# Two transformer layers on one core: part of V and of the queries made inside attention, scores first, compact reciprocals

## The chip, the cores and the metric

The kernel runs on one core of a Trainium2 chip. The metric is the device time of one execution in microseconds; the median of several runs is compared.

## The reference

Four blocks follow each other on x of 2048 positions by 1024 features: linear attention (A), softmax attention (B), then A and B again with the same weights. Each block normalises x, projects it to Q, K and V for 32 heads of 32 features, attends, projects with `wo` and adds the result to x.

```python
x = x + _A_ref(_layernorm(x), A_wqkv, A_w_phi, A_wo)
x = x + _B_ref(_layernorm(x), B_wqkv, B_wo)
x = x + _A_ref(_layernorm(x), A_wqkv, A_w_phi, A_wo)
x = x + _B_ref(_layernorm(x), B_wqkv, B_wo)
# _B_ref, per head:
scores = jnp.einsum("bhqd,bhkd->bhqk", q, k) * (Dh ** -0.5)
p = _softmax(scores, axis=-1)
o = jnp.einsum("bhqk,bhkd->bhqd", p, v)
# _A_ref, per head, with phi = [softmax(x w_phi), softmax(-x w_phi)]:
kv = phi_k^T v;  o = (phi_q kv) / (phi_q sum(phi_k))
```

x and the weights are bf16.

## The kernel before

The kernel does not issue its instructions as it goes. Each step is recorded with `op(engine, cost, function, dependences, buffers, priority)`. A planner (`Sched.run`) then plays the steps through with a cost for each, and writes them out in the order in which it started them. On the chip every engine works through its own list in that order and waits at the head for what it needs. The planner gives an engine the ready step with the lowest priority number whose buffers can be allocated: SBUF buffers come from one arena (the tile `arena`), with a quota per class (`QUOTA`), PSUM banks from eight. It looks past at most 60 steps that can't be allocated, and at most 80 units of priority ahead (`WINDOW`). A turn of attention is 10 units. A DMA is planned with 0.55 us to issue and `2.0 + kb / 200` us to land. All but two DMAs are issued from SP.

x stays in SBUF, transposed (`xT`), as four chunks of 512 positions (`NC`). "Layer" in the code means an A block and the B block behind it; `last` is the second. There are eight head groups of four heads (`G`).

The stage ahead of each B attention does, chunk by chunk, the queries and output of A (`a_queries`, `a_out`), layernorm, K of head group 0 (`b_k`) and V of head groups 0 to 3 (`b_v`, column block `fc` 0, four tiles of 128 positions; ACT evicts them). These matmuls are plain ones, 128x128 by 512 columns (line 421).

Attention (`attention`) walks 32 turns, each a chunk of queries and a head group: first chunks 0 and 1 by group, then chunk 2, then chunk 3. A turn has 64 units of 128 keys by 512 queries. Three units make one step: three score matmuls on separate row groups of the array (line 1006) into one of two PSUM score areas (three banks each), then one exponential of 128x1536 on ACT into an `E` buffer (line 1012). Scores for step n+2 need the area that step n's exponential has read. Two units make one products step (line 1042): V and a column of ones against the exponentials, four column tiles at once, accumulated in bank 6. After each half turn DVE copies bank 6 to an SBUF tile `T` (line 1057).

Some pairs of units are taken off ACT and done as a polynomial on DVE (`exp_dve`, lines 944 to 966); `EXTRA` says in which turns, one or two pairs a turn.

The rest of B's projections are *fills*, matmuls in four column tiles on bank 7 alone (`FIL`; line 425), put between attention's steps, each evicted by DVE: K of groups 1 to 7 (`b_k`), V of groups 4 to 7 (`b_v`, lines 839 and 1186), queries (`b_q`, line 847), the output projection (`b_o`, and `b_last` in the second layer), and in the first layer the keys of the next A block (`a_keys`). The queries of chunks 2 and 3 are made early, during the turns of chunks 0 and 1, from the weights loaded for those; `q_away` writes them to memory (`qd`, line 865) and `q_back` reads them shortly before their turn (lines 871 to 873). Where PE would otherwise work less than 75% of a 3.4 us spell, the planner puts in filler matmuls with a zero weight (line 1253).

The denominators of a turn come out of the ones column, equal in 32 rows per head. Two DMAs of 64x512 bring them beside each other (lines 1083 and 1085), four reciprocals of 128x128 follow on DVE (line 1087), and two products of 64x512 write the normalised output (line 1091):

```python
rc = [op("DVE", 128 * 8 / 960 + 0.12, lambda b=b, d_v=d_v, r_v=r_v: nc.vector.reciprocal(
    out=r_v()[:, b * P:(b + 1) * P], in_=d_v()[:, b * P:(b + 1) * P]), [m1, m2], [d_b], prio)
    for b in range(4)]
```

The last turn of each attention has a way of its own (lines 1064 to 1082).

Of the kernel before, what the change touches and what calls it, by code (L numbers as in the profile page):

```python
# [10 lines left out]
ACT = mybir.ActivationFunctionType  # L11
ALU = mybir.AluOpType
# [8 lines left out]
C512 = 512  # L21
# [11 lines left out]


class Op:
    __slots__ = ("eng", "dur", "lat", "fn", "bufs", "prio", "mode", "ndep", "out", "t", "start", "seq", "accum")

    def __init__(self, eng, dur, lat, fn, bufs, prio, mode, seq):
        self.eng, self.dur, self.lat, self.fn, self.bufs = eng, dur, lat, fn, bufs
        self.prio, self.mode, self.seq = prio, mode, seq  # L40
        self.ndep, self.out, self.t, self.start, self.accum = 0, [], 0.0, None, None


LAT = {"PE": 0.25, "ACT": 0.2, "DVE": 0.1, "POOL": 0.2, "SP": 2.0, "AQ": 2.0}
# [3 lines left out]
class Sched:  # L48
# [96 lines left out]
    def run(self):  # L145
# [20 lines left out]
        started = {}  # L166
        for o in self.ops:
            if o.ndep == 0:
                heapq.heappush(ready[o.eng], (o.prio, o.seq, o))
        t, left, order = 0.0, len(self.ops), []  # L170
        while left:
            moved = False
            for e in engines:
# [1 line left out]
                    continue  # L175
                skipped = []
                pick = None
                while ready[e] and len(skipped) < 60:
                    item = heapq.heappop(ready[e])
                    if item[0] <= todo[front] + WINDOW and self._alloc(item[2].bufs):  # L180
                        pick = item[2]
                        break
                    skipped.append(item)
                for s in skipped:
# [43 lines left out]
            if moved:  # L228
                continue
            if not events:  # L230
                stuck = [(o.prio, o.eng, [(b.cls, b.at) for b in o.bufs]) for e in engines for _, _, o in ready[e]][:8]
                raise AssertionError(f"nothing can start at {t:.1f}: {left} left, {stuck}, live {self.live}")
            t = events[0][0]
            while events and events[0][0] <= t + 1e-9:
                _, _, o, own = heapq.heappop(events)
                if not own:
                    for b in o.bufs:
                        b.left -= 1
                        if b.left == 0:
                            self._release(b)  # L240
                for x in o.out:

                    if own != (x.eng == o.eng and x.eng not in ("SP", "AQ")):
                        continue
                    x.ndep -= 1
                    if x.ndep == 0:
                        heapq.heappush(ready[x.eng], (x.prio, x.seq, x))
        self.end = t
        return order

# [4 lines left out]
LONG = {"kT", "v", "slab", "slabk", "xn", "xn1", "kvacc", "kvm", "zm", "wnat"}  # L255
MODEST = {"slabk", "xn1", "e1", "vp1", "pkf", "lnw1", "w2o"}
QUOTA = {"pk": 3, "pv": 2, "kv": 1, "ln": 2, "mm": 2, "cmp": 2, "bc": 4, "num": 1, "wt": 4, "fil": 2,
         "e": 6, "vp": 6, "e1": 4, "vp1": 4, "E": 5, "q2": 3, "kt": 3, "w2": 8, "w2o": 3, "oT": 26, "T": 4, "den": 2,
         "lnt": 6, "lnw": 2, "lnw1": 1, "eq": 8, "ns": 4, "cw": 6, "hl": 6, "oc": 2, "slab": 7, "slabk": 3, "fin": 4,
         "rs": 8, "pkf": 1, "part": 8, "w2r": 1,  # L260
         "xs": 1, "xu": 2, "xg": 2, "xx": 2, "E1": 3}
SPELL = 3.4
KEEP = 0.75
# [3 lines left out]
POW2_0 = 0.998010015430466  # L267
POW2_C = (-2.753493604392706, 3.611980637904819, -2.738565741928622)
LEAD = 5.0
EXTRA = (lambda i: [(i % 2, 2)] if 12 <= i < 17 else [],  # L270
         lambda i: [(0, 2), (1, 2)] if 16 < i < 30 and i % 4 else [(i % 2, 2)] if 8 <= i < 30 else [])


def act_us(n):
    return n / 1200 + 0.064


def dve_us(n):
    return n / 960 + 0.15
# [6 lines left out]
def kernel(  # L286
# [83 lines left out]
    wdq_v = wd_q[:].rearrange("(po pi) f -> pi po f", pi=P)  # L370
    wdk_v = wd_k[:].rearrange("(po pi) f -> pi po f", pi=P)

    qd = dram_p.tile([P, 2 * G * C512], BF16, tag="qd")
    qd_v = qd[:].rearrange("p (c g n) -> p c g n", c=2, g=G)
    xd = dram_p.tile([P, 3 * PO * C512], BF16, tag="xd")
# [206 lines left out]
    def flat(deps):  # L582
        r = []
        for d in deps:
            if isinstance(d, (list, tuple)):
                r.extend(flat(d))
            elif d is not None:
                r.append(d)
        return r
# [74 lines left out]
                            flat([last, kv_last.get((fc, lo))]), [pb, kv_b], pr))  # L664
                kv_last[(fc, lo)] = adds

    def mmg2(pb, pv, lhs, rhs, d1, d2, bufs, prio, lo=0, hi=4, more=False):

        last = None
        cols, us, mode = kind(pb)  # L670
        for i in range(lo, hi):
            def fn(i=i):
                for po in (2 * i, 2 * i + 1):
                    mm(pv(), lhs(po), rhs(po), po == 2 * lo, po == 2 * hi - 1 and not more, cols)
            last = op("PE", 2 * us, fn, [last] + flat([d1[i] if d1 else None, d2[i] if d2 else None]),
                      [pb, *bufs], prio, mode=mode)
        return last

# [154 lines left out]
                        in_=kv()[64 * pp:64 * pp + 64, 256 * hf:256 * hf + 256]),  # L833
                    [cp], [kb, k_b], kb=32))

    def evac(eng, dst, src, dep, bufs, prio):
        if eng == "ACT":
            return op("ACT", act_us(512), lambda: nc.scalar.copy(out=dst(), in_=src()), [dep], bufs, prio)
        return op("DVE", dve_us(512), lambda: nc.vector.tensor_copy(out=dst(), in_=src()), [dep], bufs, prio)  # L839

    def b_q(g, c, prio, w, banks):
        wb, ww, wd = w
# [29 lines left out]
            dma(prio, lambda: nc.sync.dma_start(out=q_v()[64:128, 1, :], in_=src[0:64]), [away], [q_b], kb=64),  # L872
            dma(prio, lambda: nc.sync.dma_start(out=q_v()[0:64, 1, :], in_=src[64:128]), [away], [q_b], kb=64)]

    def b_v(fc, c, t, prio, w, vT, banks, eng):
        wb, ww, wd = w
        xb, xv, fin = xnB[c]
        ts = slice(t * P, (t + 1) * P)
        pb, pv = ps("fil", banks)
        m = mmg2(pb, pv, lambda po: xv()[:, po, ts], lambda po: ww()[:, po, :], fin, wd, [xb, wb], prio)  # L880
        v_b, v_v, done = vT[(fc, c)]
        done[t] = evac(eng, lambda: v_v()[:, t, :], pv, m, [pb, v_b], prio)

    def b_o(ft, c, prio, w, oT, banks, part=None, lo=0, hi=4):

# [85 lines left out]
    def attention(base, kT, vT, q_of, gate, extra):  # L971
# [16 lines left out]
        while i < len(units):  # L988
# [14 lines left out]
            def sfn(grp=grp, s_v=s_v):  # L1003
                for x, (qc, g, pp, d, j) in enumerate(grp):
# [4 lines left out]
                        rhs=q_of[(qc, g)][1]()[r, (pp + j // 2) % 2, :],  # L1009
                        start=True, stop=True, tile_position=(32 * j, 0))  # L1010
            so = op("PE", 0.24, sfn, deps + (gate if n == 0 else []), [s_b, *bufs], prio - 2, mode="r")
            ex = op("ACT", act_us(w * C512), lambda s_v=s_v, e_v=e_v, w=w: nc.scalar.activation(  # L1012
                out=e_v()[:, 0:w * C512], in_=s_v(), func=ACT.Exp, scale=4 * math.log(2)),
                [so], [s_b, e_b], prio - 3)
# [6 lines left out]
        if True:  # L1021
            for qc, g in turns:
                T = []
                end = (qc, g) == turns[-1]
                for pp in range(2):
                    a_b, a_v = ps("acc", [(6,)])
                    last = None
                    for d in range(8):
                        prio = base + 10 * pos[(qc, g)] + 5 * pp + 0.5 * d
                        for u in range(2):  # L1030
# [17 lines left out]
                            ebs = [e_of[us[0]][0]]  # L1048
                            if e_of[us[1]][0] is not ebs[0]:
                                ebs.append(e_of[us[1]][0])  # L1050
                            last = op("PE", 0.225, fn, flat([last, ex_of[us[0]], ex_of[us[1]], v_done[kc % 4]]),
                                      [a_b, v_b, *ebs], prio - 1, mode="c")
                            last.accum = (d, u) != (7, 1)
                    if end and pp:
# [9 lines left out]
                if end:  # L1064
# [15 lines left out]
                        [ln], [o_b, l_b, a_b], prio))  # L1080
                    oTs[qc][g] = (o_b, o_v, s)
                    continue
                m1 = dma(prio, lambda d_v=d_v, T=T: nc.sync.dma_start(out=d_v()[hi_, :], in_=T[0][1]()[hi_, :]),
                         [T[0][2]], [d_b, T[0][0]], kb=128)
                m2 = dma(prio, lambda d_v=d_v, T=T: nc.sync.dma_start(out=d_v()[lo_, :], in_=T[1][1]()[lo_, :]),
                         [T[1][2]], [d_b, T[1][0]], kb=128)
                rc = [op("DVE", 128 * 8 / 960 + 0.12, lambda b=b, d_v=d_v, r_v=r_v: nc.vector.reciprocal(  # L1087
                    out=r_v()[:, b * P:(b + 1) * P], in_=d_v()[:, b * P:(b + 1) * P]), [m1, m2], [d_b], prio)
                    for b in range(4)]
                o_b, o_v = sb("oT", C512)  # L1090
                s = [op("DVE", dve_us(512), lambda a=a, b=b, k=k, o_v=o_v, r_v=r_v, T=T: nc.vector.tensor_tensor(
                    out=o_v()[a, :], in0=T[k][1]()[a, :], in1=r_v()[b, :], op=ALU.mult),
                    rc, [o_b, r_b, T[k][0]], prio)
                    for k, (a, b) in enumerate(((lo_, hi_), (hi_, lo_)))]
                oTs[qc][g] = (o_b, o_v, s)
        return oTs, so

# [25 lines left out]
    for layer in range(2):  # L1123
# [39 lines left out]
        for c in range(NC):  # L1163
            pr = second + 20 * c
            o_b, o_v = sb("oc", G, C512)
            oc = (o_b, o_v, {})
            for hf in range(2):
                a_queries(c, hf, pr + 5 * hf, wq_s, state, oc)
            a_out(c, pr + 22, wo_s, oc)
            xnB[c] = layernorm(c, pr + 23, ANY)  # L1170
            b_k(0, c, pr + 42, wk0, kT, ANY, "ACT")
            if c == 0:
                q_of[(0, 0)] = b_q(0, 0, pr + 42.5, wq0, ANY)
            for t in range(TB):
                b_v(0, c, t, pr + 43 + 0.1 * t, bv_s[0], vT, ANY, "ACT")
        gate = []
        at = second + 130

# [5 lines left out]
        for c in range(NC):  # L1184
            for t in range(TB):
                b_v(1, c, t, at + 4.5 * (4 * c + t) + 2, bv_s[1], vT, FIL, "DVE")
        for g in range(G):
            pr = at + 10 * pos[(0, g)]
            w = slab("w2", pr - 11, B_w[:, :, g * P:(g + 1) * P], P) if g else wq0
            for qc in range(NC):  # L1190
                if qc < 2:
                    if qc or g:
                        q_of[(qc, g)] = b_q(g, qc, pr + 10 * qc - 8, w, FIL)
                else:
                    away = q_away(g, qc, pr + 2 + 6 * (qc - 2), w, FIL)
                    q_of[(qc, g)] = q_back(g, qc, at + 10 * pos[(qc, g)] - 12, away)
# [92 lines left out]
```

## Time and profile before

| | us |
|---|---|
| median of 3 runs (2509.66 to 2510.57) | 2510.38 |
| the profiled execution's own time | 2511.27 |
| its span, first to last instruction | 2509.5 |
| PE, ACT, DVE busy | 2368.6, 2145.4, 1468.5 |
| exponentials of the first attention, first start and last end | 357.6 to 1343.8 |
| exponentials of the second attention | 1566.4 to 2497.5 |

In the profile, PE is TensorE's matmuls, PEld its weight loads, DVE VectorE, ACT ScalarE, SP the engine that issues the DMAs. L1012 is line 1012 of the kernel before. Matmuls are pipelined, so a busy PE is not PE at its peak; a matmul of 512 columns shows some 0.38 us, but the next one starts 0.22 us after it. Rows of waits give who waited, for whom, the total us, the number of times and the longest.

### The profile page before, as it was taken

Reading aid. Unit: us, or ns where it says so; the run is one execution under the profiler, and the core shown is the slowest. Engines: PE = TensorE matmul, PEld = TensorE weight load, DVE = VectorE, ACT = ScalarE, POOL = GpSimd, SP = SyncE. Lnnn points to the kernel's source line nnn. Section 1 sums busy time; section 2 is a strip of 40 time slices with the busy share of each in tenths; the row PEclk is TensorE's granted clock in tenths of the full one; section 3 lists DMA queues with packets and bytes.
Section 4 is the critical chain, followed back from the end, with each engine's and each line's share of the span. In section 5 each row is a group of like instructions: output and inputs, shape, how many; then the busy total and the mean of one; then the engine's idle time right before and its main releaser. Section 6 shows DMA issues by size and latency. Waiting matters only on the chain.

```text
span 2509.5 us, 62924 instructions
## 1 busy us (share of the span) xinstructions
PE 2368.6 (94%) x27872; PEld 893.4 (36%) x27872; DVE 1468.5 (59%) x2003; ACT 2145.4 (85%) x1897; POOL 26.1 (1%) x72
## 2 busy tenths in 40 slices
PE   7999999999999999999999999999999999999998
PEld 4443433333333333333333444333333333333333
DVE  6997653333356345654646766333356578687854
ACT  6335558999999999999996465699999999999998
POOL 0000000000000000000000000000000000000000
PEclk9999999999999999999999999999999999999999
DMA  9110012111121222222323001111121100110000
GB/s 219 33 44 1 22 21 48 35 36 44 41 62 42 56 54 69 77 66 69 114 65 116 1 5 38 36 36 35 40 62 27 35 27 27 29 33 27 25 25 27
DMA packets 185282, 117.39 MB, mean 47 GB/s; under 512 B 103344, under 2 KB 175024, under 8 KB 184240
## 3 DMA queue, kind: packets, MB, share of 16 engines
q1 hardware_dynamic: 183952, 111.26, 16.7%
q8 instruction: 218, 3.57, 0.6%
q10 hardware_dynamic: 1056, 2.10, 0.3%
q14 instruction: 56, 0.46, 0.1%
HBM read 62.46 MB, written 15.73 MB: 31 GB/s over the span
## 4 chain that ended last, share of the span: by engine, by line
ACT 46%; PE 31%; issue 12%; DVE 8%; SPq 1%; DMA 1%; ACTq 0%; DVEq 0%
ACT arena L1012 43%; PE psum L421 14%; PE psum L425 5%; PE psum L1042 5%; PE psum L1006 4%; DVE arena L616 1%; SPq L456 1%; PE psum L1253 1%; PE psum L780 1%; ACT arena L612 1%; DVE arena L625 1%; DVE arena L963 1%; DVE arena L662 1%; DVE arena L510 1%; DVE arena L514 1%
## 5 line engine op out<-in xcount | busy, mean ns | idle before, releaser
L1012 ACT ACTIVATE arena<-psum 128x1536 bf16<-128x1536 f32 x1342 | 1812.4, 1566 | 50.5 <-PE psum L1006 43.7
L1042 PE MATMUL psum<-arena 128*32 128x512 bf16 x4096 | 699.0, 385 | 11.6 <-ACT arena L1012 8.4
L1042 PE MATMUL psum<-arena,ones_bf 128*32 128x512 bf16 x4096 | 700.3, 386 | 0.0
L1006 PE MATMUL psum<-arena 32*128 32x512 bf16 x4022 | 522.8, 383 | 74.6 <-ACT arena L1012 68.3
L425 PE MATMUL psum<-arena 128*32 128x512 bf16 x8256 | 576.3, 380 | 4.9 <-DVE arena L625 1.3
L421 PE MATMUL psum<-arena 128*128 128x512 bf16 x2032 | 474.2, 383 | 18.1 <-DVE arena L514 5.4
L1006 PEld LDWEIGHTS <-arena 32*128 32x128 bf16 x4022 | 163.4, 91 | 574.8 <-issue 564.9
L421 PEld LDWEIGHTS <-arena 128*128 128x128 bf16 x2032 | 193.6, 98 | 265.8 <-issue 47.6
L425 PEld LDWEIGHTS <-arena 128*32 128x32 bf16 x8256 | 212.3, 96 | 209.8 <-issue 53.9
L1042 PEld LDWEIGHTS <-arena 128*32 128x32 bf16 x4096 | 165.8, 94 | 271.6 <-issue 246.5
L1087 DVE RECIPROCAL arena<-arena 128x128 f32<-128x128 f32 x248 | 212.9, 913 | 44.7 <-DMA arena<-arena 44.4
L1253 PE MATMUL psum<-xT,zero 128*32 128x512 bf16 x2712 | 218.5, 382 | 0.0
L839 DVE CAST arena<-psum 128x512 bf16<-128x512 f32 x112 | 77.3, 690 | 238.5 <-PE psum L425 238.1
L1042 PEld LDWEIGHTS <-ones_bf 128*32 128x32 bf16 x4096 | 158.4, 94 | 62.7 <-issue 50.8
L1057 DVE COPY arena<-psum 128x512 f32<-128x512 f32 x126 | 86.8, 689 | 157.3 <-PE psum L1042 155.6
L963 DVE SCALAR_TENSOR_TENSOR arena<-arena 128x1024 f32<-128x1024 f32 x111 | 135.6, 1222 | 2.3
L612 ACT ACTIVATE arena<-psum 128x512 bf16<-128x512 f32 x80 | 42.8, 600 | 86.1 <-PE psum L421 57.8
L742 ACT ACTIVATE arena<-psum 128x512 bf16<-128x512 f32 x128 | 69.8, 597 | 41.5 <-PE psum L421 32.0
L625 DVE TENSOR_TENSOR arena<-psum,arena 128x1024 bf16<-128x1024 f32 x64 | 78.3, 1224 | 39.6 <-PE psum L425 35.5
L510 DVE TENSOR_TENSOR arena<-xT,arena 128x1024 f32<-128x1024 bf16 x64 | 77.9, 1219 | 35.2 <-ACT arena L499 34.8
L1253 PEld LDWEIGHTS <-zero 128*32 128x32 bf16 x2712 | 70.3, 97 | 64.5 <-issue 16.8
L514 DVE TENSOR_TENSOR arena<-arena 128x1024 bf16<-128x1024 f32 x64 | 77.4, 1223 | 23.9 <-ACT arena L504 22.6
(100 smaller groups left out, 1428.3 us busy)
## 6 DMA issues: line engine op xcount, KB each, us to landing
arena<-arena SPq DMA_DIRECT2D x124, 128.0 KB, 2.2
arena<-in_A_wqkv_dram SPq DMA_DIRECT2D x10, 1024.0 KB, 5.5
arena<-in_B_wqkv_dram SPq DMA_DIRECT2D x32, 256.0 KB, 3.1
arena<-arena SPq DMA_DIRECT2D x256, 32.0 KB, 1.9
arena<-in_B_wo_dram SPq DMA_DIRECT2D x32, 256.0 KB, 3.0
arena<-wd_k SPq DMA_DIRECT2D x8, 1024.0 KB, 5.7
arena<-in_A_wo_dram SPq DMA_DIRECT2D x4, 1024.0 KB, 7.1
arena<-in_B_wqkv_dram SPq DMA_DIRECT2D x4, 1024.0 KB, 5.4
```

Source lines behind the costliest of these rows:

```text
L421: nc.tensor.matmul(out_, lhsT=lhsT, rhs=rhs, start=start, stop=stop, skip_group_check=True)
L425: nc.tensor.matmul(out_[ks, :], lhsT=lhsT[:, ks], rhs=rhs, start=start, stop=stop, tile_position=(0, 32 * k), skip_group_check=True)
L510: s1 = op("DVE", dve_us(1024), lambda pr=pr, w_v=w_v: nc.vector.tensor_tensor(out=w_v(), in0=xT[:, pr, csl(c)], in1=m_v().unsqueeze(1).to_ ...
L514: fin.append(op("DVE", dve_us(1024), lambda pr=pr, w_v=w_v: nc.vector.tensor_tensor(out=xv()[:, pr, :], in0=w_v(), in1=r_v().unsqueeze(1). ...
L625: ml = op("DVE", dve_us(1024), lambda vpv=vpv, wv_=wv_, sv=sv: nc.vector.tensor_tensor(out=wv_()[:, :, :, 0:DH], in0=vpv().rearrange("p (h ...
L963: last = [op("DVE", dve_us(1024), lambda i=i, c=c: nc.vector.scalar_tensor_tensor(out=x_v(), in0=(x_v() if i else g_v()), scalar=c, in1=g_ ...
L1006: nc.tensor.matmul(out=s_v()[:, x * C512:(x + 1) * C512], lhsT=kT[g][1]()[r, pp, d * P:(d + 1) * P], rhs=q_of[(qc, g)][1]()[r, (pp + j // ...
L1012: ex = op("ACT", act_us(w * C512), lambda s_v=s_v, e_v=e_v, w=w: nc.scalar.activation(out=e_v()[:, 0:w * C512], in_=s_v(), func=ACT.Exp, s ...
L1042: nc.tensor.matmul(out=a_v()[col:col + 32, :], lhsT=v_v()[:, kc % 4, o:o + DH] if what == 0 else ones_bf[:], rhs=ev()[:, x * C512:(x + 1) ...
L1057: cp = op("DVE", dve_us(512), lambda t_v=t_v, a_v=a_v: nc.vector.tensor_copy(out=t_v(), in_=a_v()), [last], [a_b, t_b], prio - 4)
L1087: rc = [op("DVE", 128 * 8 / 960 + 0.12, lambda b=b, d_v=d_v, r_v=r_v: nc.vector.reciprocal(out=r_v()[:, b * P:(b + 1) * P], in_=d_v()[:, b ...
L1253: nc.tensor.matmul(psum[32 * k:32 * k + 32, 6 * C512:7 * C512], lhsT=zero[:], rhs=xT[:, 0, 0:C512], start=False, stop=False, tile_position ...
```

## The change

In the planner, a step can be marked `first`; such steps go ahead of all others on their engine, whatever their priority. All score steps but the first two of each attention are marked. The planner now looks past 400 steps instead of 60. `E` gets six buffers instead of five.

In the second layer, V of head groups 2 and 3 (the upper 256 columns of column block 0) is no longer made in the stage ahead of attention but as fills of 256 columns, evicted by DVE; head groups 0 and 1 stay. Queries of chunks 2 and 3 are made by `b_q` shortly before their turn, with a weight load of their own, and don't go through memory. The first layer keeps both as they were.

In both layers the denominators are compacted: two DMAs pick one row of 512 per head into a 128x16 tile, one reciprocal is taken, the result goes to a memory scratch `rd`, and one DMA reads it back with each of the four rows repeated over 32 partitions. `EXTRA` is changed: pairs on DVE go from 5 to 10 in the first layer and from 32 to 34 in the second.

```diff
@@ Sched.run
-                heapq.heappush(ready[o.eng], (o.prio, o.seq, o))
+                heapq.heappush(ready[o.eng], (not o.first, o.prio, o.seq, o))
...
-                while ready[e] and len(skipped) < 60:
+                while ready[e] and len(skipped) < 400:
...
-         "e": 6, "vp": 6, "e1": 4, "vp1": 4, "E": 5, "q2": 3, ...
+         "e": 6, "vp": 6, "e1": 4, "vp1": 4, "E": 6, "q2": 3, ...
...
-EXTRA = (lambda i: [(i % 2, 2)] if 12 <= i < 17 else [],
-         lambda i: [(0, 2), (1, 2)] if 16 < i < 30 and i % 4 else [(i % 2, 2)] if 8 <= i < 30 else [])
+EXTRA = (lambda i: [(0, 2), (1, 2)] if 12 <= i < 17 else [],
+         lambda i: [(0, 2), (1, 2)] if 16 <= i < 30 else [(i % 2, 2)] if 10 <= i < 16 else [])
@@ attention
             so = op("PE", 0.24, sfn, deps + (gate if n == 0 else []), [s_b, *bufs], prio - 2, mode="r")
+            so.first = n >= 2
...
-                m1 = dma(prio, lambda d_v=d_v, T=T: nc.sync.dma_start(out=d_v()[hi_, :], in_=T[0][1]()[hi_, :]),
-                         [T[0][2]], [d_b, T[0][0]], kb=128)
-                m2 = dma(prio, lambda d_v=d_v, T=T: nc.sync.dma_start(out=d_v()[lo_, :], in_=T[1][1]()[lo_, :]),
-                         [T[1][2]], [d_b, T[1][0]], kb=128)
-                rc = [op("DVE", 128 * 8 / 960 + 0.12, ... for b in range(4)]
+                c_b, c_v = sb("cden", 16, dt=F32)
+                at_d = rd_v[len(gone)]
+                gone.append((qc, g))
+                m = [dma(prio, lambda k=k, c_v=c_v, T=T: nc.sync.dma_start(
+                    out=c_v()[64 * k:64 * k + 64, :],
+                    in_=T[k][1]()[64 * (1 - k):64 * (1 - k) + 64:32, :].rearrange("r (s c) -> r s c", c=16)),
+                    [T[k][2]], [c_b, T[k][0]], kb=4) for k in range(2)]
+                rc = op("DVE", 0.27, lambda c_v=c_v: nc.vector.reciprocal(out=c_v(), in_=c_v()), m, [c_b], prio)
+                aw = dma(prio, lambda c_v=c_v, at_d=at_d: nc.sync.dma_start(
+                    out=at_d.rearrange("h (s c) -> (h s) c", c=16), in_=c_v()), [rc], [c_b], kb=8)
+                bk = dma(prio, lambda r_v=r_v, at_d=at_d: nc.sync.dma_start(
+                    out=r_v(), in_=at_d.unsqueeze(1).to_broadcast([4, 32, C512])), [aw], [d_b], kb=256)
...
-                    rc, [o_b, r_b, T[k][0]], prio)
+                    [bk], [o_b, r_b, T[k][0]], prio)
@@ stage ahead of attention, and fills
-                b_v(0, c, t, pr + 43 + 0.1 * t, bv_s[0], vT, ANY, "ACT")
+                b_v(0, c, t, pr + 43 + 0.1 * t, bv_s[0], vT, ANY, "ACT", (0,) if last else (0, 1))
...
                 b_v(1, c, t, at + 4.5 * (4 * c + t) + 2, bv_s[1], vT, FIL, "DVE")
+                if last:
+                    b_v(0, c, t, at + 1.5 * (4 * c + t) + 3, bv_s[0], vT, FIL, "DVE", (1,))
...
+                elif last:
+                    pq = at + 10 * pos[(qc, g)]
+                    q_of[(qc, g)] = b_q(g, qc, pq - 14, slab("w2", pq - 20, B_w[:, :, g * P:(g + 1) * P], P), FIL)
                 else:
                     away = q_away(g, qc, pr + 2 + 6 * (qc - 2), w, FIL)
                     q_of[(qc, g)] = q_back(g, qc, at + 10 * pos[(qc, g)] - 12, away)
```

`b_v` and `mmg2` take the half of the columns and its share of the planned cost; the products wait for the half that holds their head group.

## The prediction

> **What bounds the kernel now.** I read the busy time by stage first, split at the edges of the two attentions (357 to 1346 us and 1566 to 2497 us). Columns: stretch, length, then busy time of PE, PEld, DVE, ACT, POOL, the granted clock, DMA.
>
> ```profile
> 392.00:617.00 225.00, 219.73 (x3122) 77.45 (x3125) 78.25 (x107) 218.50 (x163) 0.00 (x0) 1.00 0.16 39
> ...
> 1346.00:1566.00 220.00, 213.99 (x1122) 90.95 (x1121) 155.76 (x233) 115.09 (x193) 2.59 (x8) 0.98 0.07 21
> ...
> 1601.00:1769.00 168.00, 164.72 (x2356) 58.41 (x2360) 57.52 (x79) 161.92 (x121) 0.00 (x0) 1.00 0.17 40
> ...
> 2030.00:2497.00 467.00, 435.34 (x6122) 152.39 (x6122) 335.05 (x408) 465.47 (x347) 0.00 (x0) 1.00 0.10 26
> ```
>
> Late in attention ACT is busy 465.5 of 467 us; between the attentions it is busy for half the time and PE for 214 of 220. So two engines take turns as the bound: PE in the projections, ACT in attention. DVE bounds neither. The same stretches for line 1012, the exponential, alone (ACT busy, count):
>
> ```profile
> 392.00:617.00 225.00, 218.01 (x162) 1.00 0.16 39
> 617.00:900.00 283.00, 282.81 (x211) 1.00 0.20 52
> 900.00:1305.00 405.00, 372.82 (x274) 1.00 0.25 74
> ...
> 1601.00:1769.00 168.00, 161.73 (x120) 1.00 0.17 40
> 1769.00:2030.00 261.00, 255.23 (x191) 0.99 0.15 39
> 2030.00:2497.00 467.00, 465.47 (x347) 1.00 0.10 26
> ```
>
> Undisturbed, 211 exponentials take 283 us: 1.34 us each. At that pace the six rows need 217, 283, 367, 161, 256 and 465 us. Row three also holds 24 us of other ACT work (its ACT busy time over all lines is 396.56). What is left is ACT's lost time: 8, 0, 14, 7, 5 and 2 us. That is all that a better order inside attention can win. The view of waits after 1601 us names the late side:
>
> ```profile
> ACT arena L1012 <- PE psum L1006: 7.0, 11, 1.3
> ACT arena L1012 <- DMA qd<-arena: 3.6, 1, 3.6
> ```
>
> Scores are late, and once the write of a far query is. The timeline gives PE's rates (start, length, line, count; the last matmul's own 0.38 or 0.22 us is taken off):
>
> ```profile
> 131.56 0.85 PE L644 MATMUL psum<-arena 128*128 128x132 bf16 x12
> ...
> 1448.05 5.90 PE L421 MATMUL psum<-arena 128*128 128x512 bf16 x26
> ```
>
> 5.52/25 = 0.22 us (0.216 in longer rows) per 512 columns, 0.63/11 = 0.057 per 132. A straight line between them gives 0.109 for the new 256 columns (bounds 0.057 and 0.216). A step of attention's four column tiles costs the same 0.216, and going from scores to those and back about 0.1 each way.
>
> **Part by part.** The sum is made against this execution: span 2509.5, its time 2511.27, so 1.8 outside; the median of the runs is 2510.38, 0.9 below it.
>
> *Exponentials.* Pairs done on DVE rise from 37 to 44; each takes two of three units off ACT. The programs hold 1340 full and 2 one-unit exponentials before, 1336 and none after. ACT saves 4 x 1.34 + 2 x 0.75 (mean of the short form) = 6.9, less what a short one hides under its neighbour: **-6.5** (-6.9 to -6.3). Four go from the first attention.
>
> *V and its stage.* 128 matmuls of V (16 tiles x 8) halve: 128 x (0.216 - 0.109) = 13.7 us less PE work between 1346 and about 1600, and 16 ACT evictions go from 587 ns to something between 250 and 587. The other half returns as 128 four-tile steps inside attention: 128 x 0.109 = 14.0 us, its 16 evictions on DVE (0.25 to 0.69 each). PE has no slack early there: filler matmuls (line 1253), put in where PE lacks work, take only 5.3 of the 168 us after 1601. So I did not take the 13.7 whole, but summed PE's work in the order of both programs, from the last score group of the first attention to the 126th of the second: 398.6 us before, 386.4 after (plain matmuls 195.6 to 182.0, fills 69.6 to 75.2, attention's products 51.4 to 48.8, fillers 3.3 to 1.5, the rest unchanged). That is **-12**; the first three blocks of 21 groups come to 58, 30 and 30 us of PE for 28 of ACT, so the second attention begins slower than now. Bounds -4 (V was covering the chain of layernorm) and -16 (waits inside shrink too).
>
> *Queries of chunks 2 and 3.* 16 x 8 x 0.216 = 27.6 us of fills move from the first to the second half of the second attention, where fillers take 99 of 467 us: hidden; without that cover it would cost up to 27.6. Sixteen writes and 48 reads through memory go, 16 slab loads of 256 KB and 32 swaps come. The 3.6 us wait for such a write goes, and with it a stretch at half clock (1856 to 1867 us had 0.69 granted): **-4** of the 5 us lost in 1769 to 2030 (0 to -5).
>
> *Scores first, deeper search, sixth E buffer.* They can only win the lost time above. PE already waits for ACT before scores:
>
> ```profile
> L1006 PE MATMUL psum<-arena 32*128 32x512 bf16 x4022 | 522.8, 383 | 74.6 <-ACT arena L1012 68.3
> ```
>
> so where ACT is full this changes nothing. Early in the first attention PE's order sums to 3.5 us less over the first 168 groups (238.7 to 235.2): **-4** of 8 (0 to -8). In 900 to 1305, 8.2 of the 14 us are waits for scores; half of that, **-4** (+3, if products and keys come late instead, to -10). Late in the second: **-1** (0 to -2).
>
> *Compact reciprocals.* Per turn, 62 times, four reciprocals (3.65 us) become one of 128x16 (between 0.15, the smallest DVE rows, and 0.353, its 128x32 form: 0.25). DVE loses 62 x 3.4 = 211 us and gets 7 x 9.0 = 63 from the new pairs (lines 949 to 966). DVE is not the bound, so this wins nothing itself. But two copies become a chain of two small copies, the reciprocal, a write and a broadcast read back, 108 more issues on SP in all (739 to 847), and the two products then wait at DVE's head. The near rows:
>
> ```profile
> arena<-arena SPq DMA_DIRECT2D x124, 128.0 KB, 2.2
> ...
> arena<-in_B_wqkv_dram SPq DMA_DIRECT2D x32, 256.0 KB, 3.1
> ...
> arena<-in_B_wqkv_dram SPq DMA_DIRECT2D x4, 1024.0 KB, 5.4
> ...
> qd<-arena SPq DMA_DIRECT2D x32, 128.0 KB, 1.8
> ```
>
> Write and read take 0.35 + 1.8 + 0.48 + 3.1 = 5.7 us by the like rows (issue times from the same lines). The planner orders DVE for 0.55 + 2.04 + 0.55 + 3.28 = 6.4, so DVE should seldom stand; behind the products in its queue wait the fill bank's eviction and the T copy, then PE's next fill, then scores, and ACT has up to two scored groups (2.7 us) in hand. Now DVE stands 44.4 us for such copies, unnoticed. **+3** for one or two reads that meet the 1 MB weight loads and land 5 us late, less the cover (0 to +12, five of them).
>
> The Trainium skill ("DMA: Bandwidth & Descriptors", How many engines (k), under the section on the semaphore's 16) speaks against this read: the slowest dimension of either side sets how many of the 16 queues work, and the source has 4 rows there. That would put 64 KB on each of 4 queues, as the 1 MB load does on 16, so an estimate by it is 5.4 us in place of 3.1 and 8.0 for the trip: 1.6 us later than ordered, still inside the cover, and the sum would stay. No run shown has a read of this shape.
>
> **Sum.** -6.5 - 12 - 4 - 4 - 4 - 1 + 3 = -28.5: span 2481.0, with 1.8 outside 2482.8, and 0.9 less for the median: **2482**.
>
> **Rivals.**
> *The reciprocal's trip holds DVE (slower).* It decides once write and read pass 6.4 + 2.7 = 9.1 us, that is a read over about 6.5. For: 1 MB loads reach 7.2, one 128 KB write took 7.9, and with few fills one eviction stands right behind the products. Against: like sizes land in 3.1. If the read took 8 us throughout, each of 62 turns would be 1.5 us beyond the cover, 93 us, and PE's waits would bring half clock: 2482 + 90 = 2572 (2530 if half the turns pay). The Trainium skill's rule of 4 queues, above, gives 5.4 by itself, short of that point. Chance 0.11.
> *The projection stage is a chain.* If layernorm's ACT and DVE steps, not PE, end last, V's half buys 2 us instead of 12: 2492. Against: PE is busy 136.88 of 137 us between 1428 and 1565. 0.12.
> *Scores first does not do what it says*, since in-order PE and two score banks already set the pace: the 4 + 4 + 1 fall away: 2491. For: 68.3 us of score waits for ACT. 0.13.
> *All lost time goes*, at the far bounds: about 2466. For: the rows of waits that must vanish come to 8.2 + 7.0 + 3.6 us. 0.08.
> *Gains and new waits cancel*, 2507 to 2513: 0.03.
> The forecast itself, 2472 to 2490: 0.53.
>
> **Numbers.** Bounds added up: best -6.9 - 16 - 5 - 8 - 10 - 2 = -48, 2462; worst -6.3 - 4 + 0 + 0 + 3 + 0 + 12 = +5, 2514. That leaves out the first rival and little else. No change means within 0.2%, 5 us, about what a measurement of this kernel can tell. Below 2505: 0.53 + 0.12 + 0.13 + 0.08, less 0.03 for their upper ends = 0.83; within 0.03; above 0.14.
>
> **What would show it.** Right: the stage between the attentions some 20 us shorter, the second attention's first 126 exponentials no faster, exponentials 1336 at 1.34 us, the wait on qd gone, ACT's waits for scores below 15 us in all. Wrong: DVE's products waiting long for the read with PE waiting for DVE; a read landing over 6 us; gaps of PE in the projections.

## The result, and the profile after

The changed kernel takes **2857.66 us** (median of 4 runs, 2850.91 to 2860.57) against 2510.02 of the kernel before in the same session (2509.13 to 2510.57). The ratio is 1.1382 [1.1361, 1.1402]: 348 us slower, where 28 us faster was forecast. Its profiled execution has a span of 2854.8 us.

The busy time by stage of the changed kernel, in the columns of the prediction (length, PE, PEld, DVE, ACT, POOL, granted clock, DMA):

```profile
392.00:617.00 225.00, 195.83 (x2681) 67.08 (x2680) 48.07 (x74) 192.71 (x142) 0.00 (x0) 0.96 0.13 34
617.00:900.00 283.00, 235.51 (x2903) 74.28 (x2897) 113.90 (x152) 231.96 (x171) 0.00 (x0) 0.90 0.15 40
...
1520.00:1722.00 202.00, 191.15 (x1029) 84.90 (x1046) 141.76 (x215) 107.44 (x182) 2.58 (x8) 0.98 0.09 26
...
2030.00:2497.00 467.00, 383.56 (x4732) 122.09 (x4731) 213.44 (x274) 381.55 (x279) 0.00 (x0) 0.90 0.12 32
```

No engine is full any more inside attention. In the last row ACT is busy 381.6 of 467 us, where it was 465.5, with PE at 383.6. The stage between the attentions (third row) is the part that came out as forecast: 202 us, from the start of the last exponential to that of the next, for 223 before. The exponentials themselves are not slower (a mean of 1473 ns, 1566 before). The page's groups show where the time lies (busy us and mean ns, then idle time before them and what ended it). First the exponentials of the kernel before, then exponentials and score matmuls of the changed one:

```profile
L1012 ACT ACTIVATE arena<-psum 128x1536 bf16<-128x1536 f32 x1342 | 1812.4, 1566 | 50.5 <-PE psum L1006 43.7
```

```profile
L1023 ACT ACTIVATE arena<-psum 128x1536 bf16<-128x1536 f32 x1336 | 1829.9, 1473 | 389.6 <-DMA arena<-arena 267.5
L1015 PE MATMUL psum<-arena 32*128 32x512 bf16 x4008 | 555.3, 405 | 313.1 <-ACT arena L1023 307.2
```

ACT stands idle 389.6 us before its exponentials (50.5 in the kernel before), and 267.5 of that ends with a DMA from the arena to the arena. An exponential reads PSUM and writes an `E` buffer; none of its data passes through such a DMA. The line whose DMA it is, asked for by itself, names the culprit. Line 1098 is the pair of compact copies, and these are the instructions that waited for it (us, times):

```profile
L1098 SPq DMA_DIRECT2D arena<-arena x124: 507/549/624, 401.4 to 2815.6; - x124
...
  ACT arena L1023: 267.5, 118
  DVE arena L1102: 68.1, 29
  DVE arena L842: 63.1, 20
```

Only line 1102, the reciprocal, has business with that copy. The exponentials and line 842, DVE's eviction of K and V, write other buffers of the arena. The views of waits, of the engines and of the DMA queue, show both halves:

```profile
ACT arena L1023 <- DMA arena<-arena: 267.5, 118, 7.8
```

```profile
SPq L1098 <- ACT arena L1023: 80.1, 89, 3.9
```

In 89 cases the copy is issued only when the exponential ahead of it has ended, and in 118 the next exponential starts only when the copy has landed. The timeline shows one such stop, SP first, then ACT:

```profile
704.58 0.56 SPq L1098 DMA_DIRECT2D arena<-arena  x1
```

```profile
699.08 5.48 ACT L1023 ACTIVATE arena<-psum 128x1536 bf16<-128x1536 f32 x4
706.51 5.48 ACT L1023 ACTIVATE arena<-psum 128x1536 bf16<-128x1536 f32 x4 [1.96 <-DMA arena<-arena]
```

ACT ends at 704.56, the copy is issued at 704.58, and ACT starts again 1.96 us later. The compact copies are barriers for other buffers of the arena. In the instruction lists of the two programs the same can be counted without a run: 118 exponentials of the changed kernel wait for the copy issued directly ahead of them, with no other exponential between. In the kernel before, the exponentials that wait for line 1083 or 1085 have at least five others between, as buffers that are used again must have.

### The profile page after: what moved, and what is told of

Same layout as the page of the kernel before. It is cut to its first block, busy times and chain, and to the rows that moved or that the text cites. A ratio compares the mean times of both kernels' runs of the same rounds, so it can differ in the third digit from the quotient of the medians.

```text
span 2854.8 us, 62275 instructions
## 1 busy us (share of the span) xinstructions
PE 2436.4 (85%) x27419; PEld 892.3 (31%) x27484; DVE 1336.3 (47%) x1903; ACT 2161.3 (76%) x1891; POOL 24.9 (1%) x72
## 5 line engine op out<-in xcount | busy, mean ns | idle before, releaser
L1023 ACT ACTIVATE arena<-psum 128x1536 bf16<-128x1536 f32 x1336 | 1829.9, 1473 | 389.6 <-DMA arena<-arena 267.5
L1015 PE MATMUL psum<-arena 32*128 32x512 bf16 x4008 | 555.3, 405 | 313.1 <-ACT arena L1023 307.2
L1053 PE MATMUL psum<-arena 128*32 128x512 bf16 x4096 | 705.9, 410 | 13.4 <-DVE arena L1068 8.2
L428 PE MATMUL psum<-arena 128*32 128x512 bf16 (+1 forms) x8768 | 638.3, 395 | 24.5 <-DVE arena L842 16.9
L424 PE MATMUL psum<-arena 128*128 128x512 bf16 (+1 forms) x1975 | 454.4, 375 | 23.5 <-DVE arena L1089 4.1
L424 PEld LDWEIGHTS <-arena 128*128 128x128 bf16 x2032 | 193.2, 98 | 256.6 <-issue 52.5
L842 DVE CAST arena<-psum 128x512 bf16<-128x512 f32 (+1 forms) x128 | 84.0, 657 | 375.4 <-PE psum L428 307.2
L1275 PE MATMUL psum<-xT,zero 128*32 128x512 bf16 x2064 | 183.2, 417 | 0.0
L1108 DVE TENSOR_TENSOR arena<-arena 64x512 bf16<-64x512 f32 x124 | 84.9, 685 | 108.2 <-DMA arena<-rd 77.0
L958 DVE TENSOR_SCALAR arena<-psum 128x512 f32<-128x512 f32 x88 | 60.7, 689 | 112.0 <-PE psum L953 84.9
L619 DVE TENSOR_REDUCE arena<-arena 128x32 f32<-128x1024 bf16 x64 | 77.7, 1214 | 51.5 <-ACT arena L615 46.2
L850 DVE TENSOR_SCALAR arena<-psum 128x512 bf16<-128x512 f32 x48 | 33.1, 690 | 146.6 <-PE psum L428 110.6
L745 ACT ACTIVATE arena<-psum 128x512 bf16<-128x512 f32 x128 | 69.8, 598 | 41.1 <-PE psum L424 31.5
L628 DVE TENSOR_TENSOR arena<-psum,arena 128x1024 bf16<-128x1024 f32 x64 | 78.0, 1218 | 38.8 <-PE psum L428 28.3
```

What stands on the lines that cost most here:

```text
L424: nc.tensor.matmul(out_, lhsT=lhsT, rhs=rhs, start=start, stop=stop, skip_group_check=True)
L428: nc.tensor.matmul(out_[ks, :], lhsT=lhsT[:, ks], rhs=rhs, start=start, stop=stop, tile_position=(0, 32 * k), skip_group_check=True)
L619: red = op("DVE", dve_us(1024), lambda ev=ev, sv=sv: nc.vector.reduce_sum(out=sv(), in_=ev().rearrange("p s (h d) -> p (s h) d", d=DH), ax ...
L628: ml = op("DVE", dve_us(1024), lambda vpv=vpv, wv_=wv_, sv=sv: nc.vector.tensor_tensor(out=wv_()[:, :, :, 0:DH], in0=vpv().rearrange("p (h ...
L842: return op("DVE", dve_us(n), lambda: nc.vector.tensor_copy(out=dst(), in_=src()), [dep], bufs, prio)
L1015: nc.tensor.matmul(out=s_v()[:, x * C512:(x + 1) * C512], lhsT=kT[g][1]()[r, pp, d * P:(d + 1) * P], rhs=q_of[(qc, g)][1]()[r, (pp + j // ...
```

## The experiments

The theory: the source of a compact copy, two rows 32 partitions apart (`[... :64:32, :]`), is taken by the dependence tracking for all arena memory that lies between them. Whatever is written there then waits, and the copy waits for whatever was being written. Two rivals stood beside it: 124 small DMAs more cost this by themselves, or the trip through memory does.

**One-row copies.** Each strided copy becomes two copies of one row.

```diff
-                out=c_v()[64 * k:64 * k + 64, :],
-                in_=T[k][1]()[64 * (1 - k):64 * (1 - k) + 64:32, :]...
-                [T[k][2]], [c_b, T[k][0]], kb=4) for k in range(2)]
+                out=c_v()[64 * k + 32 * h:64 * k + 32 * h + 32, :],
+                in_=T[k][1]()[64 * (1 - k) + 32 * h:64 * (1 - k) + 32 * h + 1, :]...
+                [T[k][2]], [c_b, T[k][0]], kb=2) for k in range(2) for h in range(2)]
```

> The change, with each small copy that picks two rows 32 partitions apart (one DMA, 124 in all) split into two that pick one row each (248). Theory A: the copy whose source steps over 32 partitions is taken by the dependence tracking for all the memory between its rows, so the next exponential, whatever buffer it writes, is made to wait until it lands, and it waits for the one before; one-row copies aren't. Then the 118 waits of the exponential for such a copy (267.5 us) go, and the time falls to the prediction's 2482, within 2470 to 2500. Theory B: the write and broadcast read hold DVE's products, and PE behind them: unchanged trip, so 2830 to 2870. Theory C: many small DMAs on SP are slow by themselves: twice as many copies, so 2860 or more.

Measured: 2508.87 us, ratio 1.0008 [0.9998, 1.0018]. With twice as many copies 349 us are gone, so the strided source was the loss. But the forecast's gain is not there either: the time lies above the 2470 to 2500 of theory A.

**The strided copies alone, and plain ones in their place.** The kernel before, and after each turn two copies that nothing reads: the strided ones, and in the second kernel 64 neighbouring partitions by 16 elements, the same 4 KB.

```diff
+                c_b, c_v = sb("cden", 16, dt=F32)
+                for k in range(2):
+                    dma(prio, lambda k=k, c_v=c_v, T=T: nc.sync.dma_start(
+                        out=c_v()[64 * k:64 * k + 64, :],
+                        in_=T[k][1]()[64 * (1 - k):64 * (1 - k) + 64:32, :]...    # strided
+                        in_=T[k][1]()[64 * (1 - k):64 * (1 - k) + 64, 0:16]),     # plain
+                        [T[k][2]], [c_b, T[k][0]], kb=4)
```

> The kernel before, with the two strided copies of the change added per turn into a tile that nobody reads; all else as before. Theory A: two barriers a turn cost what they cost in the change, about 124 x 2.8 = 347 us: 2800 to 2900. Theory B: no broadcast read, no product waits for one: 2505 to 2515. Theory C: 124 small copies more on SP, which has room: 2510 to 2530.

> As the run with the strided copies added to the kernel before, but each copy takes 64 neighbouring partitions by 16 elements: the same bytes, the same number of DMAs, the same tile. Theory A: no barrier, 2505 to 2520. Theory C: the same cost as the strided ones.

Measured: strided 2843.6 us, ratio 1.134 [1.1317, 1.1364]; plain 2512.0, ratio 1.0019 [1.0009, 1.003]. With nothing else of the change present, the strided copies cost 336 us, nearly the whole loss of 348, and 124 DMAs more cost 2 to 8 us by the interval. The strided copies are not slow themselves: by the updates of their semaphores in the trace they land 1.8 us after their issue begins, the plain ones 1.9. In the view of waits of the strided kernel the same stop stands at the exponential:

```profile
ACT arena L1012 <- DMA arena<-arena: 232.5, 109, 8.0
```

In the plain one no exponential waits for such a DMA. What remained open was the missing 28 us.

**The read in four parts.** The one-row version, with the broadcast read made as four DMAs, each of one row into 32 partitions. In the one-row version the view of waits had

```profile
DVE arena L1108 <- DMA arena<-rd: 116.9, 41, 8.0
```

```diff
-                bk = dma(... out=r_v(), in_=at_d.unsqueeze(1).to_broadcast([4, 32, C512])), [aw], [d_b], kb=256)
+                bk = [dma(... out=r_v()[32 * h:32 * h + 32, :],
+                    in_=at_d[h:h + 1, :].to_broadcast([32, C512])), [aw], [d_b], kb=64) for h in range(4)]
```

> The run with one-row copies, and the broadcast read split into four DMAs, each one row to 32 partitions. Theory D, with few queues for a source of four rows: the read, 4.5 us from issue to the products, comes down to 2.5 to 3, DVE's 117 us of standing for it fall below 70, and the time to 2490 to 2502. Theory E: DVE stands less, the time stays within 3 us of the one-row run. If three more issues on SP (0.5 us each) cost what the landing gains: no change in either.

Measured: **2479.65 us**, ratio 0.9889 [0.9873, 0.9904]: 28.3 less than before, the forecast's gain, and better than the 2490 to 2502 of theory D. (Its profiled execution, of span 2474.7, lies 3 us under this median.) DVE's products now wait a third as long (they are line 1109 here), ACT's idle time before the exponentials falls from 64.3 to 39.1 us, and the page gives a landing for the parts:

```profile
DVE arena L1109 <- DMA arena<-rd: 38.3, 29, 6.1
```

```profile
arena<-rd SPq DMA_DIRECT2D x248, 64.0 KB, 2.0
```

Whether the total is right for the forecast's reasons is another matter. The next runs undo its parts one by one, first on the one-row version with the slow read, then on this one.

**The reciprocals of before** in the changed kernel, with five `E` buffers. (With six, this kernel gave no result.)

> The change with the reciprocals of before (two copies of 64x512, four reciprocals of 128x128) and five E buffers, as these take more room; scores first, V and queries inside attention, pairs on DVE all as changed. Theory D: with the barrier gone, the rest of the forecast gain is eaten by the reciprocal's trip (DVE stood 117 us for the read in the run with one-row copies): 2478 to 2492. Theory E: it is eaten by V and fills that crowd the start of the second attention, and by waits in the projection stage: 2500 to 2512.

Measured: 2506.67 us, ratio 0.9996 [0.9987, 1.0005]. With five `E` buffers and the new reciprocals (below) it is 2483.46, so here the old ones cost 23 us. The number is theory E's, but not for its reason, as V and the fills are the same in the two kernels. Both have started 420 exponentials of the second attention when the next starts at 2147.3 us. The next 283 us of the two (old reciprocals, then new; PE, PEld, DVE, ACT):

```profile
2147.00:2430.00 283.00, 261.61 (x3705) 91.79 (x3693) 245.51 (x297) 260.82 (x194) 0.00 (x0) 1.00 0.10 24
```

```profile
2147.00:2430.00 283.00, 260.13 (x3582) 91.20 (x3578) 211.30 (x265) 282.85 (x212) 0.00 (x0) 0.99 0.10 26
```

212 exponentials against 194, 18 x 1.34 = 24 us. In this stretch the exponentials of the kernel with the old reciprocals stood 22 us, none of it for a DMA:

```profile
ACT arena L1023 <- PE psum L1053: 15.5, 12, 2.6
ACT arena L1023 <- DVE arena L975: 6.6, 1, 6.6
```

Line 1053 is the products, which read the `E` buffers, and line 975 the last step of a polynomial on DVE. The other kernel has no such row here. So with the pairs and fills of the change on top, DVE at 245.5 of 283 us was late for the others; which of its steps held the products is not shown.

**The planner of before** on the one-row version: no scores first, depth 60, five `E` buffers.

```diff
-            so.first = n >= 2
...
-                while ready[e] and len(skipped) < 400:
+                while ready[e] and len(skipped) < 60:
...
-... "E": 6, ...
+... "E": 5, ...
```

> The run with one-row copies, but no scores first, the planner looking past 60 steps and five E buffers, as before. By the forecast these three are worth 9 us: 2514 to 2522. If in-order PE and the score areas set the pace whatever the order: within 3 us of the one-row run. If scores first crowds fills and products out: faster than the one-row run by 5 or more.

Measured: 2535.74 us, ratio 1.0111 [1.0097, 1.0125], 26.9 over the one-row version, three times the forecast's 9.

**V of groups 2 and 3 ahead of attention again**, on the one-row version.

```diff
-                b_v(0, c, t, pr + 43 + 0.1 * t, bv_s[0], vT, ANY, "ACT", (0,) if last else (0, 1))
+                b_v(0, c, t, pr + 43 + 0.1 * t, bv_s[0], vT, ANY, "ACT", (0, 1))
...
-                if last:
-                    b_v(0, c, t, at + 1.5 * (4 * c + t) + 3, bv_s[0], vT, FIL, "DVE", (1,))
```

> The run with one-row copies, but V of head groups 2 and 3 made ahead of attention, as before. By the forecast its move is worth 12 us: 2517 to 2524. Theory E: it only moves the work from one place where PE bounds to another: within 3 us of the one-row run.

Measured: 2496.77 us, ratio 0.9957 [0.9944, 0.9969]. With the slow read, moving V costs 12.1 us.

**The same undoings on the version with the read in four parts** (2479.65 us), with the edits shown above; for the queries `elif last:` becomes `elif False:`.

> The version with one-row copies and the read in four parts (2479.7 us, 1336 exponentials), and V of head groups 2 and 3 made ahead of the second attention again, as before. On the version with the slow read this gained 12.1 us (2508.9 to 2496.8). Theory A, the move of V costs by itself, because its 14 us of matmuls and 16 evictions fall where PE has no slack: about 2468. Theory B, V's evictions on DVE only cost where DVE stood for the slow read, and the forecast's 12 us saved come out with the fast one: about 2492. Theory C, the two cancel: 2477 to 2482.

Measured: 2477.44 us, ratio 0.9878 [0.9864, 0.9891]; 2.2 less, and the two intervals overlap.

> The version with one-row copies and the read in four parts (2479.7 us), without scores first, with the search depth of 60 and five E buffers. On the version with the slow read this cost 26.9 us. Theory A, scores first and the sixth buffer are worth that whatever the read: about 2507. Theory B, they mostly covered the wait for the slow read, and are worth the forecast's 9 without it: about 2489.

Measured: 2499.51 us, ratio 0.9967 [0.9955, 0.998], 19.9 more, between the two theories.

> The version with one-row copies and the read in four parts (2479.7 us), and the queries of chunks 2 and 3 of the second layer made early and kept in memory again, as before. Forecast: the wait on that write (3.6 us) comes back and nothing else, about 2484 (0 to 5 more). Rival: early in the second attention PE has no slack, and the 27.6 us of fills there cost in earnest: 2490 to 2507.

Measured: 2483.88 us, ratio 0.9905 [0.989, 0.992], 4.2 more; here too the two intervals overlap. The forecast's number came out, but not what it was to come from: no exponential of this run waits for a DMA to or from `qd`.

**Which planner edit**, on the same version: only the mark `first` away, and only the sixth `E` buffer away.

> The version with one-row copies and the read in four parts (2479.7 us), only the mark that puts scores first taken away; depth 400 and six E buffers stay. All three together are worth 20 us there. Theory A, scores first makes it: 2497 to 2502. Theory B, a buffer or the depth makes it: 2480 to 2485.

Measured: 2498.41 us, ratio 0.9958 [0.9945, 0.997], 18.8 more.

> The version with one-row copies and the read in four parts (2479.7 us), with five E buffers instead of six; scores first and depth stay. Theory A, scores first makes the 20 us: 2480 to 2484. Theory B, the sixth buffer: 2495 to 2500.

Measured: 2483.46 us, ratio 0.9901 [0.9885, 0.9916], 3.8 more, with overlapping intervals. The mark makes nearly all of it. ACT's waits for scores, without it and with it:

```profile
ACT arena L1022 <- PE psum L1015: 48.4, 37, 14.0
```

```profile
ACT arena L1023 <- PE psum L1015: 29.1, 8, 14.0
```

48.4 - 29.1 = 19.3 us, where the two profiled spans (2496.4 and 2474.7) differ by 21.7. The exponentials' waits for products rose with the mark, from 2.8 to 9.1 us, so the two numbers don't match exactly. Of the waits for scores that are left, 14.0 is a single one.

**The compact reciprocals alone** on the kernel before, with one-row copies and the read in four parts; V, queries, planner and pairs as before.

> The kernel before (1340 full exponentials, its own order of V, queries and planner) with the compact reciprocals alone, one-row copies and the read in four parts: DVE loses 62 x 3.4 = 211 us, but is not the bound. Forecast (+3, 0 to +12): 2511 (2508 to 2520). Rival, DVE's evictions and T copies hold PE now and then, so lighter reciprocals gain: 2490 to 2503.

Measured: 2506.37 us, ratio 0.9987 [0.9978, 0.9996]: 2.7 less, outside both ranges.

## Why the prediction was wrong, step by step

**The step that failed** is the cost of the compact reciprocals, "+3 (0 to +12)". It summed a trip of four transfers by their sizes and asked when DVE's products would stand. The two compact copies were taken as small DMAs of 4 KB. What they cost lies outside that sum: each is a barrier at which the exponentials stop, 349 us by the one-row version, 336 by the strided copies alone on the kernel before. No row of the trace of before could give that price, since no copy there had such a source; but the instruction lists of the changed kernel hold the waits, 118 of them, and the prediction did not read them.

**The first rival** had the right part of the change and the wrong mechanism. It put the delay in the read and DVE: 90 us for a read of 8 us, and a loss only from a read over 6.5 us, or a trip over 9.1. The read of four rows in one DMA did cost time, short of that point. Where DVE's products ended up waiting for it in the one-row version, they started 5.0 us (4.7 to 8.1) after its issue began; in four parts the median is 3.3 from the start of the first issue. The page counts a landing from the start of the issue, so the like row's 3.1 is what compares with these 5.0, and the forecast's sum of the trip, 5.7, holds the two issues twice. From the reciprocal's end to products that waited, the one-row version took 8.0 us in the median (6.2 to 11.1), 1.6 later than the planner orders DVE. By the prediction that was still inside the cover of 2.7 us, ACT's two scored groups, and would cost nothing. It cost 2508.87 - 2479.65 = 29 us: the products stood for 78.6 us more in sum (116.9 - 38.3), and ACT 25 us more before its exponentials (64.3 - 39.1). So the cover was not there when it counted. (The prediction's upper bound, too, adds up to 2515, not 2514.)

The Trainium skill ("DMA: Bandwidth & Descriptors", How many engines (k), under the section on the semaphore's 16) put only 4 queues on that read, and the estimate by it was 5.4 us for the landing. The trace agrees: by the semaphore's updates the read landed 4.9 us after its issue began, above the 3.1 of the like row and below the estimate. Where each DMA of the kernel before leaves 16 updates on its semaphore, this read leaves 5, one after 1.0 us and four near its landing. By the same rule the four parts, with 32 rows on both sides, would have 16 queues each; each leaves 16 updates, and they land in 2.0 us for 64 KB.

**The other terms**, against the run that undoes each on the version with the fast read, and the reciprocals in both places where they were run:

| term | forecast, us | measured, us |
|---|---|---|
| V and the start of the second attention | -12 | +2, not told from 0 |
| queries without memory | -4 | -4, intervals overlap |
| scores first, depth, sixth buffer | -9 | -20, the mark alone -19 |
| compact reciprocals, as repaired | +3 | -3 alone on the kernel before, -23 within the change (five `E` buffers) |
| exponentials fewer | -6.5 | not run by itself |

The terms are not independent: with the forecast's -6.5 they add to -31.5 by the first number of the reciprocals and to -51.5 by the second, and the repaired kernel stands at -28.3. That the forecast's total matches that version is luck: V was 14 us too good, scores first 11 too poor, and the reciprocals were priced as a cost where they gained.

**V.** PE's sum in order, 398.6 to 386.4 us, was put down to the wrong edit. By its own parts, plain matmuls fell by 13.6, as V's half says. Fills rose by only 5.6, although V's half alone adds 14.0: the other 8.4 had left with the queries of chunks 2 and 3. For V alone the two ends cancel. On the fast read it is so: from the start of the last exponential of the first attention until the first 126 of the second are done, it takes 418.5 us with V moved (1321.7 to 1740.2) and 417.0 without (1324.2 to 1741.2). The stage is 22 us shorter, and the first 126 exponentials take 217.2 us instead of 193.2. With the queries made early again the same stretch takes 424.1. In the kernel before it took 426.3, so both moves together won 8 us there, not 12. A 256-column matmul measured 0.109 us, as taken from the line between two rows: 16 in 1.91 us,

```profile
1530.15 1.91 PE L424 MATMUL psum<-arena 128*128 128x256 bf16 x16 [0.46 <-ACT arena L841]
```

(1.91 - 0.27)/15. So the price was right and the owner wrong.

**Queries.** Their -4 was forecast from a wait on the write to `qd` and a dip of the clock behind it. With the queries back in memory that wait did not return. What grew was the stretch just named, by 5.6 us, which speaks for the other side of the move: fewer fills early in the second attention, a gain that the forecast held inside V's sum. The size was right by luck.

**Scores first** was taken at half the lost time of two stretches of the first attention, 8 us, and at 1 us in the second. By the profiles without and with the mark it won 14.5 us in the first attention (980.8 to 966.3) and 6.6 in the second (945.5 to 938.9). It won also where the forecast had not looked: the stages shown began at 392 us, and the first 21 exponentials from 357 us on take 56.7 us without the mark and 52.4 with it. The rival "all lost time goes", given 0.08, had this term's size (8 + 10 + 2 = 20), though not all lost time went: 39.1 us of idle time before the exponentials are left.

**What was to be seen** came true in part: a stage some 20 us shorter, no faster first 126 exponentials (203.0 us before, 246.7 after, 217.2 in the repaired version), 1336 exponentials in all, and none of the repaired version waiting on `qd`. ACT's waits for scores did not fall below 15 us: they are 69.5 in the changed kernel and 29.1 in the repaired one. Of the signs named for "wrong", products waiting long for the read did appear, 77.0 us in the changed kernel, but they were the smaller loss.

**The version that beats both** is the changed kernel with one-row copies and the read in four parts, 2479.65 us; with V left ahead of attention it is as good, 2477.44.

## What to carry to other kernels

Before pricing a new DMA by its size, read in the built program which instructions wait for it and which it waits for: a wait of an instruction that shares no data with it is a cost that no duration shows. Copy rows that lie far apart in partitions one by one, or in one block. When a sum over both programs gives a gain, split it by edit before naming its owner, and check that work put into a full stage is smaller than what left it.

## What the runs showed that was not expected

- Two rows 32 partitions apart as the source of one DMA held up writes into other buffers of the same tile, 118 exponentials among them. That it is the tracking's description of such a source is inferred from who waits, and from the plain copy of as many bytes, which held up none.
- The stops cost more than themselves: 348 us in all, where the exponentials' waits for the copies come to 267.5. The granted clock fell to 0.90 in two of the stages shown, and the score matmuls' mean rose from 383 to 405 ns.
- Lighter reciprocals won 3 us on the kernel before and 23 in the changed one. Here the same edit was worth more once other edits had filled the engine, at 87% busy in the stretch shown.
